# Attention steps placed relative to the next unit, and weight preparation with three raw buffers and stores issued by GpSimd

## Chip, cores and metric

One core of a Trainium2 chip runs the whole program in a single launch. The metric is the time of one execution on the device in microseconds (us). The engines are called PE (TensorE, the matrix multiplications), PEld (its weight loads), DVE (VectorE), ACT (ScalarE), POOL (GpSimd) and SP (SyncE, which issues most of the DMA transfers).

## What is computed

```python
# pooled attention: 8 batches, 8 heads, 576 positions, head size 64
k_p = k.reshape(B, H, Sp, pool, D).mean(axis=3)        # pool = 8, Sp = 72
v_p = v.reshape(B, H, Sp, pool, D).mean(axis=3)
scores = scale * np.matmul(q, k_p.transpose(0, 1, 3, 2))
scores = scores - np.max(scores, axis=-1, keepdims=True)
attn = np.exp(scores)
attn = attn / (np.sum(attn, axis=-1, keepdims=True) + 1e-09)
x = np.matmul(attn, v_p)                               # to 4608 tokens x 512
# layer 1: 512 -> 2048 -> 512
r = np.maximum(x @ w_in, 0.0)
x = (s * (r * r) + b) @ w_out
# layer 2: 512 -> 1536 -> 512
gate = 1.0 / (1.0 + np.exp(-(x @ w_gate)))
out = (gate * (x @ w_val)) @ w_out2
```

The activations are float32, the weights of the two layers float64.

## The kernel before

**Precision.** A matmul of two float32 operands is made from three: each operand is split (`split`, lines 53 to 56) into a high part, copied by ACT (line 55), and the remainder, subtracted by DVE or POOL (line 56). The float64 weights come in as pairs of 32-bit words into a tile `raw` and are turned into float32 by `convert` (lines 79 to 90): one ACT instruction (line 86) and three DVE instructions (87 to 89), into a tile `cv`.

**Tokens.** There are nine blocks of 512 tokens. Attention works in 18 units of 256 tokens, two units a block. Blocks 0, 1, 2, 4 and 6 go through layer 1 in the *plain stage*: 80 steps, 16 chunks of hidden features for each block. Blocks 3, 5, 7, 8 go through layer 1 in two *paired stages* of two blocks each, in which seven products replace eight (the scheme of Winograd, with sums of weights and of activations made beforehand). Layer 2 then has four paired stages of 1024 tokens and a last narrow one of 512 (products of 256 columns).

**The plain stage** (lines 636 to 663). Step i has two half-steps, positions 2i and 2i + 1. The first runs its events, then the 12 matmuls of `emit_h` (into PSUM tile `hps`, lines 215 to 217); the second runs its events, then the 12 matmuls of `emit_x` (into `acc`, lines 243 to 245). What the events are is written out by hand with `at(position, function, ...)` in lines 476 to 521 and kept in order of insertion. From step 16 on PE and SP execute strictly in the order of the program; before that, and on ACT, DVE and POOL throughout, a planner orders the instructions before the run by a simulation of its own, and each engine's queue is then executed in that order. Unit u begins at

```python
    def pos(u):
        return (2, 16)[u - 2] if u < 4 else 32 + 39 * (u - 4) // 5
```

so that from unit 4 on units begin 8 half-steps apart, and every fifth time 7. For a unit that begins at p, `scores` of its first 128 tokens stand at p, of the second 128 at p + 4, each as two calls with a PSUM tile `sps` each (line 379, read by DVE, lines 386 and 387). `norm` (DVE and POOL) and `left` follow. `turn` transposes the probabilities with two PSUM tiles, `tm` (line 431) and `tl` (line 437): for the first 128 tokens at p + 6, for the second at p + 9. `values` multiplies by the pooled values in two halves, PSUM tile `pv` (lines 449 to 452), at p + 11 and p + 12. A half is read by ACT and DVE, which split it in place into `xh` and `xl` (line 463) where the block stays in the plain stage, or by ACT alone, which copies it into `xo` (line 457) where the block goes to a paired stage. `sps`, `tm`, `tl` and `pv` come all from the pool `ps_c`, which has two buffers that are used in turn.

**Preparation of weights.** `prep_w1` reads a chunk of layer 1's converted weights from `w6d`, lets POOL make the four sums (lines 197 to 200) and stores them: 8 chunks, all in the plain stage, at positions 40 + 8m and 44 + 8m. `prep_w2` does a chunk of layer 2 in five parts: load gate and value weights; convert the gate weights; convert the value weights and let POOL make four sums (line 181); load the output weights; convert and split them. Each part leaves its stores in a list `later`, which `store_later` issues on SP afterwards (line 149). The raw tile of the gate weights holds the sums, that of the output weights the split ones, so they are free only when their store has landed. Four chunks (`EARLY`) are done in the plain stage with three raw tiles, at 42 + 20m and every four positions from there. The other eight are done in the paired stages of layer 1 with two raw tiles: `prep_next(1)` (lines 677 to 681) is called after each half of a group and at every fourth step of what follows, 40 times in all, one part each.

**Paired stages** (lines 818 to 865). A group has 7 products of 6 matmuls: four in `first_half` (`pb` and `pc` in PSUM, additions `add2` on DVE into `wk`, line 714), three in `second_half`, then the second layer's products into `acc` (line 804). The weights of a group, tile `w`, are fetched by SP (line 692, two buffers) from `w6d` or `w7d` when the group two before it has ended, and split by ACT and POOL (lines 55, 56). A paired stage of layer 1 has 8 groups and then 16 further steps of 12 matmuls for its second block; `gen_x` meanwhile prepares the activations of the next stage, with loads that POOL issues (line 601). In these stages PE alone is in the program's order.

## Time and profile before

| | |
|---|---|
| runs of the kernel (us) | 1794.96, 1791.48, 1795.73; median 1794.96 |
| the profiled execution's own time (us) | 1793.3 |
| its span, first to last instruction (us) | 1791.4 |
| busy (us): PE, PEld, DVE, ACT, POOL | 1726.3, 1440.6, 999.9, 874.5, 689.4 |
| mean granted clock of TensorE | 0.984 of full speed |
| first product of the first and second paired stage of layer 1, of layer 2 (us) | 635.33, 800.33, 972.74 |
| moved by DMA | 347.01 MB, 194 GB/s in the mean |

A matmul is pipelined: its busy time overlaps the next one's, so the pace is read from the starts. A wait that the profile lists is idle time of an engine, put down to the instruction whose signal came last. Idle time counts for the end only where PE, which is busy for 96% of the span, has it.

### The profile page before, as it was taken

To read this page: it belongs to the slowest core of one execution; us is meant where nothing else is said; L and a number is where in the kernel's file an instruction comes from. 1 tells how busy PE (TensorE), PEld (TensorE's weight loads), DVE (VectorE), ACT (ScalarE), POOL (GpSimd) and SP (SyncE) were. 2 spreads that over 40 slices of the span, in tenths; PEclk is the share of its full clock that TensorE was granted. 3 is DMA by queue.
4 is the path that set the end of the run, shared out by engine and by line. 5 is a ranking of instruction groups with operands and counts; after the bars stand their busy time and mean duration, and the time that the engine had idled before them with its cause. 6 is when DMAs were issued, how large, how long until landed. Compare 5 with 4: busy or idle time off the path is not lost.

```text
span 1791.4 us, 22829 instructions
## 1 busy us (share of the span) xinstructions
PE 1726.3 (96%) x8184; PEld 1440.6 (80%) x8184; DVE 999.9 (56%) x1621; ACT 874.5 (49%) x1628; POOL 689.4 (38%) x756
## 2 busy tenths in 40 slices
PE   5889999999999999999999999999999999999999
PEld 4777788787788887887788888888888888888898
DVE  7997546655533477468636545454545444554354
ACT  2667555555555676536544444344434443444244
POOL 3664335455201065425431443143314331433264
PEclk7999999999999999999999999999999999999999
DMA  6866467878334477497557333733373337333753
GB/s 237 295 231 223 170 210 276 308 258 306 125 128 129 133 267 259 169 321 259 196 194 272 108 115 139 254 112 118 137 255 114 118 135 256 115 118 130 255 183 121
DMA packets 99457, 347.01 MB, mean 194 GB/s; under 512 B 11408, under 2 KB 16528, under 8 KB 99344
## 3 DMA queue, kind: packets, MB, share of 16 engines
q1 hardware_dynamic: 95120, 331.92, 53.2%
q0 software_dynamic: 4224, 13.64, 2.4%
q8 instruction: 65, 1.06, 0.2%
q14 instruction: 48, 0.39, 0.1%
HBM read 278.40 MB, written 67.11 MB: 193 GB/s over the span
## 4 chain that ended last, share of the span: by engine, by line
PE 56%; DMA 2%; DVE 1%; POOL 1%; issue 1%; ACT 0%; SPq 0%; POOLq 0%; ACTq 0%; DVEq 0%
PE acc L804 24%; PE pc L708 6%; PE pc L709 6%; PE pc L710 6%; PE pb L710 4%; PE pb L709 4%; PE pb L708 4%; DMA raw<-in 1%; DMA w<-w7d 1%; POOL w L56 1%; DMA w<-w6d 0%; DMA w7d<-raw 0%; DVE wk L714 0%; POOL raw L181 0%; DVE cv L89 0%
## 5 line engine op out<-in xcount | busy, mean ns | idle before, releaser
L56 POOL TENSOR_TENSOR w<-w 128x256 fp32r<-128x256 f32 (+1 forms) x380 | 372.8, 1015 | 601.1 <-ACT w L55 590.1
L714 DVE TENSOR_TENSOR wk<-pc,wk 128x512 f32<-128x512 f32 (+1 forms) x304 | 196.4, 646 | 320.7 <-PE pc L710 320.0
L708 PE MATMUL pc<-xo,w 128*128 128x512 f32 (+1 forms) x608 | 227.9, 375 | 4.7 <-DVE wk L714 4.4
L709 PE MATMUL pc<-xo,w 128*128 128x512 f32 (+1 forms) x608 | 227.0, 373 | 0.0
L710 PE MATMUL pc<-xo,w 128*128 128x512 f32 (+1 forms) x608 | 226.9, 373 | 0.0
L55 ACT ACTIVATE w<-w 128x256 fp32r<-128x256 f32 (+1 forms) x380 | 157.6, 491 | 107.5 <-DMA w<-w7d 91.8
L56 DVE TENSOR_TENSOR gl<-g,gh 128x512 fp32r<-128x512 f32 (+1 forms) x172 | 132.6, 771 | 103.7 <-ACT gh L55 97.3
L708 PE MATMUL pb<-xo,w 128*128 128x512 f32 (+1 forms) x456 | 170.0, 373 | 2.2 <-ACT g L737 2.0
L710 PE MATMUL pb<-xo,w 128*128 128x512 f32 (+1 forms) x456 | 170.2, 373 | 1.4 <-POOL w L56 1.4
L709 PE MATMUL pb<-xo,w 128*128 128x512 f32 (+1 forms) x456 | 169.7, 372 | 0.0
L55 ACT ACTIVATE gh<-g 128x512 fp32r<-128x512 f32 (+1 forms) x172 | 105.7, 615 | 124.3 <-DVE g L729 121.8
L804 PE MATMUL acc<-wo,s 128*128 128x512 f32 x648 | 149.7, 389 | 0.0
L804 PEld LDWEIGHTS acc<-wo,s 128*128 128x128 f32 x648 | 121.4, 188 | 25.8 <-ACT eo L810 0.4
L708 PEld LDWEIGHTS pc<-xo,w 128*128 128x128 f32 x608 | 114.9, 189 | 27.8 <-DVE wk L714 7.7
L215 PE MATMUL hps<-xl,wi 128*128 128x512 f32 (+1 forms) x328 | 133.3, 407 | 3.5 <-ACT wi L55 2.5
L804 PE MATMUL acc<-wo,gh 128*128 128x512 f32 x432 | 133.1, 389 | 0.0
L243 PE MATMUL acc<-gl,wo 128*128 128x512 f32 x320 | 130.0, 406 | 2.0 <-DVE gl L56 1.8
L710 PEld LDWEIGHTS pc<-xo,w 128*128 128x128 f32 x608 | 114.9, 189 | 20.2
L709 PEld LDWEIGHTS pc<-xo,w 128*128 128x128 f32 x608 | 115.0, 189 | 19.6
L216 PE MATMUL hps<-xh,wi 128*128 128x512 f32 (+1 forms) x328 | 129.4, 395 | 0.0
L217 PE MATMUL hps<-xh,wi 128*128 128x512 f32 (+1 forms) x328 | 129.4, 395 | 0.0
L245 PE MATMUL acc<-gh,wo 128*128 128x512 f32 x320 | 126.5, 395 | 0.0
(123 smaller groups left out, 3410.4 us busy)
## 6 DMA issues: line engine op xcount, KB each, us to landing
wo<-wo2d SPq DMA_DIRECT2D x108, 512.0 KB, 3.5
w<-w7d SPq DMA_DIRECT2D x60, 896.0 KB, 4.4
raw<-in SPq DMA_DIRECT2D x68, 512.0 KB, 5.1
wi<-w1d SPq DMA_DIRECT2D x64, 512.0 KB, 3.9
wo<-wo1d SPq DMA_DIRECT2D x64, 512.0 KB, 4.9
w<-w6d SPq DMA_DIRECT2D x16, 896.0 KB, 5.4
kv<-in SPq DMA_DIRECT2D x24, 512.0 KB, 6.3
kv<-in SPq DMA_DIRECT2D x16, 576.0 KB, 7.3
```

The costliest lines, as they stand in the source:

```text
L55: nc.scalar.activation(out=hi, in_=src, func=ACTF.Copy)
L56: eng.tensor_tensor(out=lo, in0=src, in1=hi.bitcast(F32), op=ALU.subtract)
L215: nc.tensor.matmul(out=ps[:, f], lhsT=hi[:, kk], rhs=c[:, kk, f], start=kk == 0, stop=False)
L216: nc.tensor.matmul(out=ps[:, f], lhsT=hi[:, kk], rhs=a[:, kk, f], start=False, stop=False)
L217: nc.tensor.matmul(out=ps[:, f], lhsT=lo[:, kk], rhs=a[:, kk, f], start=False, stop=kk == KD - 1)
L243: nc.tensor.matmul(out=acc[j][d], lhsT=hi[:, f], rhs=gl, start=m == 0, stop=False)
L245: nc.tensor.matmul(out=acc[j][d], lhsT=lo[:, f], rhs=gh, start=False, stop=m == M1 - 1)
L708: nc.tensor.matmul(out=ps, lhsT=w[:, 0, x, kk], rhs=r[:, 1, kk, :n], start=first and kk == 0, stop=False, skip_group_check=True)
L709: nc.tensor.matmul(out=ps, lhsT=w[:, 0, x, kk], rhs=r[:, 0, kk, :n], start=False, stop=False, skip_group_check=True)
L710: nc.tensor.matmul(out=ps, lhsT=w[:, 1, x, kk], rhs=r[:, 0, kk, :n], start=False, stop=kk == 1, skip_group_check=True)
L714: nc.vector.tensor_tensor(out=o, in0=ps, in1=b_, op=ALU.add)
L804: nc.tensor.matmul(out=a, lhsT=l, rhs=r, start=m == 0 and first == 0, stop=m == M - 1 and first == 2)
```

## The change

The attention steps of a unit u from 4 on are placed by the beginning of unit u + 1: the second `turn` at pos(u + 1) + 1, the halves of `values` at pos(u + 1) + 3 and + 5. For units 2 and 3 the second half of `values` moves from p + 12 to p + 13. `prep_w2` is taken apart into `prep_load`, `prep_gate`, `prep_val` and `prep_out`. In the plain stage one chunk of layer 2 follows two of layer 1 in a period of 22 half-steps. In the paired stages there are three raw tiles, `wk` has nine buffers instead of ten, a chunk takes four calls (33 in all), its loads are issued two calls or more before they are converted, and POOL issues the 32 stores directly after the work that they store.

```diff
--- before.py
+++ after.py
@@ -164,41 +164,49 @@
 
     prep = {}
 
-    def prep_w2(m, part):
+    def prep_load(m, what):
+        if m < M2:
+            prep[what] = load64({"g": w_gate, "v": w_val, "o": w_out2}[what][m])
+
+    def prep_gate(m):
+        prep["gt"] = convert(prep["g"], cv_tile())
+
+    def prep_val(m):
         h0, h1 = slice(0, 256), slice(256, 512)
+        gt, vt, r = prep["gt"], convert(prep["v"], cv_tile()), prep["g"].bitcast(F32)
+        s1, s2, s3, s4 = (r[:, 256 * x:256 * x + 256] for x in range(4))
+        for o, a, b_, op in ((s1, vt[:, h0], vt[:, h1], ALU.add), (s2, s1, gt[:, h0], ALU.subtract),
+                             (s3, gt[:, h0], vt[:, h0], ALU.subtract), (s4, gt[:, h1], s2, ALU.subtract)):
+            nc.gpsimd.tensor_tensor(out=o, in0=a, in1=b_, op=op)
+        stores((w7d[m][:, 512:1024], gt), (w7d[m][:, 0:512], vt), (w7d[m][:, 1024:2048], r))
+
+    def prep_out(m):
+        t = prep["o"].rearrange("p (two f) -> p two f", two=2)
+        split(t[:, 0].bitcast(F32R), t[:, 1].bitcast(F32R), convert(prep["o"], cv_tile()), nc.gpsimd)
+        stores((wo2d[m], t))
+
+    in_pairs = []
+
+    def stores(*pairs):
+        if not in_pairs:
+            later.extend(pairs)
+            return
+        for dst, t in pairs:
+            nc.gpsimd.dma_start(out=dst, in_=t if t.dtype == F32 else t.bitcast(F32))
+
+    def prep_w1(m, part):
+
         if part == 0:
-            prep["g"] = load64(w_gate[m])
-            prep["v"] = load64(w_val[m])
-        elif part == 1:
-            prep["gt"] = convert(prep["g"], cv_tile())
-            later.append((w7d[m][:, 512:1024], prep["gt"]))
-        elif part == 2:
-            gt, vt, r = prep["gt"], convert(prep["v"], cv_tile()), prep["g"].bitcast(F32)
-            later.append((w7d[m][:, 0:512], vt))
-            s1, s2, s3, s4 = (r[:, 256 * x:256 * x + 256] for x in range(4))
-            for o, a, b_, op in ((s1, vt[:, h0], vt[:, h1], ALU.add), (s2, s1, gt[:, h0], ALU.subtract),
-                                 (s3, gt[:, h0], vt[:, h0], ALU.subtract), (s4, gt[:, h1], s2, ALU.subtract)):
-                nc.gpsimd.tensor_tensor(out=o, in0=a, in1=b_, op=op)
-            later.append((w7d[m][:, 1024:2048], r))
-        elif part == 3:
-            prep["o"] = load64(w_out2[m])
-        else:
-            t = prep["o"].rearrange("p (two f) -> p two f", two=2)
-            split(t[:, 0].bitcast(F32R), t[:, 1].bitcast(F32R), convert(prep["o"], cv_tile()), nc.gpsimd)
-            later.append((wo2d[m], t))
-
-    def prep_w1(m, part):
-
-        if part == 0:
-            prep["w"] = rawp.tile([128, 1024], I32, tag="raw", name="raw").bitcast(F32)
-            nc.sync.dma_start(out=prep["w"], in_=w6d[m][:, 0:1024])
+            prep[m] = rawp.tile([128, 1024], I32, tag="raw", name="raw").bitcast(F32)
+            nc.sync.dma_start(out=prep[m], in_=w6d[m][:, 0:1024])
             return
-        v0, v1, g0, g1 = (prep["w"][:, 256 * x:256 * x + 256] for x in range(4))
+        w = prep.pop(m)
+        v0, v1, g0, g1 = (w[:, 256 * x:256 * x + 256] for x in range(4))
         nc.gpsimd.tensor_tensor(out=v1, in0=v0, in1=v1, op=ALU.add)
         nc.gpsimd.tensor_tensor(out=v0, in0=g0, in1=v0, op=ALU.subtract)
         nc.gpsimd.tensor_tensor(out=g0, in0=v1, in1=g0, op=ALU.subtract)
         nc.gpsimd.tensor_tensor(out=g1, in0=g1, in1=g0, op=ALU.subtract)
-        later.append((w6d[m][:, 1024:2048], prep["w"]))
+        later.append((w6d[m][:, 1024:2048], w))
 
     g_t = {}
 
@@ -506,19 +514,25 @@
             if t == 0:
                 at(p + 6, turn, u, 0, 0)
                 at(p + 6, turn, u, 0, 1)
-        at(p + 9, turn, u, 1, 0)
-        at(p + 9, turn, u, 1, 1)
+        later_p = p + 8 if u < 4 else pos(u + 1)
+        at(later_p + 1, turn, u, 1, 0)
+        at(later_p + 1, turn, u, 1, 1)
         at(p + 8, load_q, u + 2)
-        at(p + 11, values, u, 0)
-        at(p + 12, values, u, 1)
-
-    for m in range(M1 // 2):
-        for x in range(2):
-            at(40 + 8 * m + 4 * x, prep_w1, m, x)
+        at(later_p + 3, values, u, 0)
+        at(later_p + 5, values, u, 1)
+
     EARLY = M2 // 3
     for m in range(EARLY):
-        for x in range(5):
-            at(42 + 20 * m + 4 * x, prep_w2, m, x)
+        p = 40 + 22 * m
+        for x in range(2):
+            at(p + 2 * x, prep_w1, 2 * m + x, 0)
+            at(p + 2 * x + 4, prep_w1, 2 * m + x, 1)
+        at(p + 8, prep_load, m, "g")
+        at(p + 8, prep_load, m, "v")
+        at(p + 12, prep_gate, m)
+        at(p + 13, prep_load, m, "o")
+        at(p + 15, prep_val, m)
+        at(p + 19, prep_out, m)
 
     def probs(u, t):
         scores(u, t, 0, True)
@@ -670,15 +684,16 @@
         w7p = ctx.enter_context(tc.tile_pool(name="w7p", bufs=2, reuse_waits="tile"))
         wo2p = ctx.enter_context(tc.tile_pool(name="wo2p", bufs=4, reuse_waits="tile"))
         g2p = ctx.enter_context(tc.tile_pool(name="g2p", bufs=1, reuse_waits="tile"))
-        wk = ctx.enter_context(tc.tile_pool(name="wk", bufs=10, reuse_waits="tile"))
-        rawp = ctx.enter_context(tc.tile_pool(name="rawp2", bufs=2, reuse_waits="tile"))
-        prepare = [(m, x) for m in range(EARLY, M2) for x in range(5)]
-
-        def prep_next(n):
-            store_later()
-            for m, x in prepare[:n]:
-                prep_w2(m, x)
-            del prepare[:n]
+        wk = ctx.enter_context(tc.tile_pool(name="wk", bufs=9, reuse_waits="tile"))
+        rawp = ctx.enter_context(tc.tile_pool(name="rawp2", bufs=3, reuse_waits="tile"))
+        in_pairs.append(1)
+        prepare = [[(prep_load, EARLY, x) for x in "gvo"]]
+        for m in range(EARLY, M2):
+            prepare += [[(prep_gate, m)], [(prep_val, m)], [(prep_load, m + 1, "g")], [(prep_out, m), (prep_load, m + 1, "v"), (prep_load, m + 1, "o")]]
+
+        def prep_next():
+            for fn, *args in prepare.pop(0) if prepare else []:
+                fn(*args)
 
         w7, wo2, g2 = {}, {}, {}
 
@@ -833,14 +848,14 @@
                 for x in new(m):
                     fetch_wo((p, 0, x))
                 half = first_half(p, m)
-                prep_next(1)
+                prep_next()
                 while len(ready) >= 2:
                     outputs(ready.pop(0))
                 if m == G - 1 and kept:
                     fetch_wo(kept.pop(0))
                     fetch_wo(kept.pop(0))
                 second_half(p, m, *half)
-                prep_next(1)
+                prep_next()
                 ready += new(m)
                 if m < G - 1:
                     fetch_w7(part + 2)
@@ -856,7 +871,7 @@
             for m in range(rest):
                 split_kept(p, m + 2)
                 if m % 4 == 0:
-                    prep_next(1)
+                    prep_next()
                 emit_o(p, m, 1)
                 wo2.pop((p, 1, m))
                 if kept:
```

## Rows read from the trace of the kernel before

**Rows 1.** The page: busy time of the engines; granted clock in 40 slices.

```profile
PE 1726.3 (96%) x8184; PEld 1440.6 (80%) x8184; DVE 999.9 (56%) x1621; ACT 874.5 (49%) x1628; POOL 689.4 (38%) x756
...
PEclk7999999999999999999999999999999999999999
```

**Rows 2.** Stages in windows: length, busy time (instructions) of each engine, clock, DMA share, GB/s.

```profile
160.00:595.00 435.00, 418.12 (x2160) 351.88 (x2159) 217.93 (x411) 239.23 (x424) 155.95 (x194) 0.99 0.59 205
635.33:800.33 165.00, 164.12 (x721) 134.90 (x720) 111.73 (x158) 94.94 (x166) 75.80 (x74) 1.00 0.74 254
800.33:972.74 172.41, 166.61 (x721) 135.73 (x720) 111.47 (x158) 94.11 (x163) 68.89 (x68) 0.99 0.68 234
972.74:1152.40 179.66, 179.66 (x794) 148.60 (x792) 89.43 (x134) 73.08 (x140) 59.82 (x68) 1.00 0.45 155
...
450.00:500.00 50.00, 45.96 (x232) 38.92 (x232) 23.91 (x48) 26.46 (x49) 9.83 (x13) 0.93 0.39 136
```

**Rows 3.** Waits of PE, 160 to 595 us: total us, times, longest us.

```profile
PE sps L379 <- DVE xl L56: 11.6, 6, 4.0
PE sps L379 <- ACT xo L457: 2.1, 6, 0.4
```

**Rows 4.** Timeline of PE: start, us, what [idle before it and releaser].

```profile
439.28 0.28 PE L452 MATMUL pv<-t,v 128*128 128x256 f32 x1
...
473.83 0.28 PE L452 MATMUL pv<-t,v 128*128 128x128 f32 x1
...
478.69 1.30 PE L379 MATMUL sps<-kbd,qT 128*128 128x144 f32 x4 [4.04 <-DVE xl L56]
479.62 0.80 PE L215 MATMUL hps<-xl,wi 128*128 128x512 f32 x1
...
484.13 0.40 PE L243 MATMUL acc<-gl,wo 128*128 128x512 f32 x1
```

**Rows 5.** Timeline of PE, 212 to 218 us.

```profile
212.63 0.50 PE L243 MATMUL acc<-gl,wo 128*128 128x512 f32 x1
...
217.08 0.22 PE L449 MATMUL pv<-t,v1h 128*128 128x128 f32 x1
```

**Rows 6.** Timeline of DVE: the writes of `xl`.

```profile
442.28 0.69 DVE L56 TENSOR_TENSOR xl<-pv,xh 128x512 fp32r<-128x512 f32 x1
...
477.86 0.69 DVE L56 TENSOR_TENSOR xl<-pv,xh 128x512 fp32r<-128x512 f32 x1
```

**Rows 7.** Waits of PE, 634 to 974 us.

```profile
PE pc L708 <- DVE wk L714: 4.4, 3, 2.8
```

**Rows 8.** The chain that ended last, 855 to 864 us: start, us, what.

```profile
856.74 4.28 DMA raw<-in
...
861.54 0.61 DVE wk L714
...
862.19 0.80 PE pc L708
```

**Rows 9.** DMA issues, 600 to 975 us: count, KB each, median us to landing.

```profile
w<-w6d SPq DMA_DIRECT2D x16, 896.0 KB, 5.4
raw<-in SPq DMA_DIRECT2D x24, 512.0 KB, 4.3
...
w7d<-raw SPq DMA_DIRECT2D x8, 512.0 KB, 4.7
```

**Rows 10.** DMA issues of POOL at line 601: ns min/median/max, first and last start.

```profile
L601 POOL DMA_DIRECT2D cv<-x2d x40: 536/536/556, 931.9 to 1673.1; - x40
```

**Rows 11.** Instruction groups of POOL and ACT, 635 to 974 us: busy us, mean ns, idle before.

```profile
L56 POOL TENSOR_TENSOR w<-w 128x512 fp32r<-128x512 f32 x34 | 46.1, 1378 | 91.9 <-ACT w L55 91.9
...
L55 ACT ACTIVATE w<-w 128x512 fp32r<-128x512 f32 x33 | 19.0, 623 | 17.7 <-DMA w<-w6d 15.7 <-DMA w<-w7d 2.0
```

**Rows 12.** Windows of the instructions on `raw` alone: DVE, ACT, POOL, clock, DMA.

```profile
635.00:710.00 75.00, 22.18 (x28) 7.94 (x12) 16.09 (x15) 1.00 0.78 266
710.00:775.00 65.00, 1.00 (x1) 0.00 (x0) 0.00 (x0) 1.00 0.62 213
```

## The prediction

> **What bounds the kernel now.** I read the page's engine line first: PE is busy 1726.3 us of the span, and the granted clock is in its top tenth in all slices but the first [rows 1]. So time can only come from the places where PE stands still or runs at half clock, and the stage table says where these are [rows 2]. Layer 2 is the yardstick: 792 matmuls of 512 columns in 179.66 us, PE busy throughout, 0.2268 us each. A paired stage of layer 1 has 8 x 42 + 2 x 16 x 12 = 720 of them, 163.3 us at that rate. The first takes 165.0 and the second 172.41: they lose 1.7 and 9.1 us, 10.8 together. The plain stage from 160 to 595 us has PE busy for 418.12 of 435 us. The first 160 us and the last narrow stage lose time too, but the change hardly touches them.
>
> The waits of PE in the plain stage have one main entry: `sps`, the scores, waits for a reader of `pv`: 11.6 us in 6 waits where the block is split in place (`xl`, line 56), 2.1 us in 6 where it is only copied (`xo`, line 457) [rows 3]. Twelve waits, about one for each unit: that is a pattern of the order, not chance. Scores and values share the two PSUM buffers of `ps_c` in turn. With `pos` 8 half-steps apart, the second values half of unit u stands at p + 12, which is the next unit's p' + 4, where its second scores stand too; values come first, so the second score tile needs the buffer that the values have just filled. With 7 apart it is the first values half that lands there. The longest case is in the timeline: last values matmul at 473.83, score tile four matmuls later, then 4.04 us of idle until `xl` has been written, 477.86 + 0.69 [rows 4, 6].
>
> Some of these waits cost twice. After the 4.04 us one, twelve matmuls take from 479.62 to 484.13, 4.51 us instead of 2.72; after a shorter one, 212.63 to 217.08, 4.45 us [rows 4, 5]. The mean granted clock from 450 to 500 us is 0.93 [rows 2], that is some 7 us at the lower of its two levels, 1.2 GHz, and PE had stood idle just before. The two cost 1.8 + 1.7 = 3.5 us.
>
> In the paired stages PE waits 4.4 us for `wk` [rows 7]. The chain shows the cause: a load of `raw` of 4.28 us, the conversion's line 87 on VectorE, behind it in the same queue the `wk` addition, then `pc` at 862.19 [rows 8]. VectorE waits in order for a raw load that could only start when a store had given the buffer free. Both stages do their sixteen half-group preparations early: `raw` is worked on for 22.18 us of VectorE in 635 to 710 us and 1.00 us in 710 to 775 [rows 12], so the static order runs them at the pace of the loads.
>
> **The change, part by part.**
>
> *Values and the last turn moved.* Values halves now stand at p' + 3 and p' + 5, the turn at p' + 1; scores have p' and p' + 4, the other turn p' + 6. No half-step has values and scores together any more. Removed: 11.6 + 2.1 = 13.7 us of waits and 3.5 us of half clock, 17.2. What is late next: the second score tile at p' + 4 now needs the first values half of p' + 3, and the small transpose at p' + 6 needs the second half of p' + 5. Each has one half-step of twelve matmuls (2.72 us) and about 0.5 us of its neighbours before it, 3.2 us. How long an eviction takes, from the end of the last values matmul to the end of `xl`: 474.11 to 478.55 is 4.4 us, 439.56 to 442.97 is 3.4 [rows 4, 6]; a copied block never waits over 0.4 us [rows 3], so its evictions are shorter. So 1.2 + 0.2 us stay, and for six split units meeting a conversion's VectorE work I add 1 us: 2.5 back. Bounds: nothing gained if every wait only changes its place, 17.2 if none stays. I take -14.7, near the upper end, since only two of the evictions read exceed 3.2 us. For units 2 and 3 only the second values half moves, by one half-step, in a stretch where PE's order is not written by hand: between -2.7 and +2.7 us, taken as 0.
>
> *Early preparation laid out anew.* The same 8 `w6d` loads, 12 weight loads, 24 stores and conversions, now one after the other instead of two interleaved series, each read four half-steps or more after its load (4 x 2.72 = 10.9 us, against the 4.3 us that a raw load takes to land in the paired stages [rows 9]). All still goes through SP. None of its work ended a wait of PE in the list of the plain stage [rows 3], except through VectorE's queue, counted above. 0, with a half-step, 2.7 us, to either side.
>
> *Three raw buffers and the new steps.* Each load now stands two calls or more ahead of its conversion, with a buffer of its own. Program order has 7.5 us between calls, so two calls are 15 us. The tightest is the gate: the store of the sums must land (4.7 us) and then the load (4.3 us): 9.0 us [rows 9]. At the program's pace that fits and the 10.8 us go. But the present order runs these calls in 75 us instead of 120 [rows 12], that is 4.7 us each, and two of those are 9.4: hardly any margin. The bounds are 0 and -10.8 (a loss is a rival below). I take -6, just over half: of three loads per chunk two have ample lead and one hasn't.
>
> *Stores from GpSimd.* 8 chunks x 4 = 32 stores leave SP's queue, where they stood ahead of the raw loads. GpSimd issues its own loads in 536 ns, without spread [rows 10]: 32 x 0.54 = 17 us of an engine that is busy 75.80 + 68.89 of 337 us [rows 2]. No cost, as long as GpSimd's weight splits stay in time. Their slack: `w` lands 5.4 us after its fetch [rows 9], ScalarE's 0.62 and GpSimd's 1.38 us follow [rows 11], 7.4 us before the first product, out of a group of 66 x 0.2268 = 15.0 us. So GpSimd may be held for 7.6 us.
>
> The Trainium skill, "SBUF — State Buffer", in "SBUF: two separate sides" and the section on the wrong bandwidth intuition behind it, says that a DMA issued by GpSimd can't have its descriptors written while VectorE runs an operation that takes both ports, and gives 620 ns alone against about 3100 ns beside one. By that, 32 stores would hold GpSimd for 99 us, an estimate from the page. No run here shows it: the 40 issues of that row end at 556 ns, and few lie beside a conversion.
>
> *`wk` with nine buffers.* A group uses six, so a buffer comes round after one and a half groups, 22 us; the readers are done within one. 0. The third raw buffer takes its space.
>
> *Sum.* -14.7 - 6 = -20.7 us. The profiled execution took 1793.3 us (span 1791.4 and 1.9 around it), which gives 1772.6. The median of the runs is 1.7 us above that execution, so I forecast **1774 us**.
>
> **The rivals.**
>
> *Only the half-steps help.* The static order again follows the loads as closely as it can, and VectorE's queue meets unfinished loads as before. For: preparation packed into 75 us. Against: a third buffer and no store in the loads' queue. 1795 - 14.7 = 1780 us.
>
> *Only the preparation helps.* The waits for `pv` pass to the transposes and to the second scores, which also share `ps_c`. For: the two evictions over 3.2 us. Against: all others are shorter. 1795 - 6 to - 11 = 1784 to 1789 us.
>
> *Nothing to measure.* Both of these fail, or the gain is given back in the reordered first 160 us: 1790 to 1800 us.
>
> *Slower: GpSimd becomes late.* The place is the weight split of line 56 in layer 1, behind stores and their data in GpSimd's queue. It decides when GpSimd is held for more than 7.6 us after a group's fetch. A sum that waits for VectorE's conversion, three more sums behind it and the stores of their result, held until VectorE leaves the ports free, could do that. If half of the 16 groups come 4 us late, PE loses 32 us, and 1774 + 32 + the 6 us not gained is 1812 us. For: GpSimd's queue is in order, and it already waits for ScalarE. Against: it is idle for over half of these stages. A smaller excess gives 1801 or so.
>
> **How the numbers follow.** About 0.3%, 5.4 us, is what a measurement of this kernel can tell from no change. Chances: the forecast, with its own range of 1763 to 1780 us, 0.47; half-steps alone 0.20; preparation alone 0.12; nothing 0.12; slower 0.09. The first three lie under 1789.6: faster 0.79, same 0.12, slower 0.09. The range reaches from 1763, by 1795 - 17.2 - 10.8 - 3 = 1764, where every wait goes and the early stretch gives 3 us more, to 1788, leaving out the last two cases.
>
> **What would show it.** Right: in the list of PE's waits the entries `sps` on `xl` and `xo` are gone or under 3 us; the half-clock stretches near 213 and 480 us are missing; the first pair stage begins about 15 us earlier; the second takes nearer to 166 than 172 us; GpSimd's stores stay near 0.54 us. Wrong: `tl` or `sps` waiting for `pv` readers with 10 us or more, `pc` waiting for `wk` behind line 87 as before, or `pb` waiting for GpSimd's line 56 in layer 1.

## The result, and the profile after

The changed kernel takes 1777.85 us in the median of four runs (1777.2 to 1779.04), the kernel before 1795.35 (1791.48 to 1798.54): a ratio of 0.9904, 95% interval 0.9884 to 0.9925. The forecast was 1774 us, within 1763 to 1788, faster. The profiled execution took 1777.24 us (span 1775.4, mean clock 0.988), 16.1 us less than that of before.

The stages in windows, kernel after; the columns are those of [rows 2], and the windows of the paired stages again run from first product to first product:

```profile
160.00:595.00 435.00, 429.70 (x2236) 363.20 (x2235) 230.15 (x433) 253.87 (x452) 156.22 (x197) 1.00 0.63 215
613.51:783.12 169.61, 165.79 (x722) 134.44 (x721) 121.50 (x166) 96.25 (x168) 88.84 (x97) 1.00 0.73 254
783.12:955.10 171.98, 165.63 (x722) 136.04 (x721) 104.20 (x150) 92.66 (x161) 70.92 (x77) 0.99 0.67 226
955.10:1135.02 179.92, 179.83 (x793) 148.61 (x792) 88.94 (x134) 73.13 (x140) 60.34 (x68) 1.00 0.45 155
```

The same 435 us of the plain stage now hold 429.70 us of busy PE instead of 418.12, and the granted clock is 1.00 instead of 0.99. The first product of the paired stages comes at 613.51 us, 21.8 us earlier than the 635.33 of before. That is the whole gain and more. The two paired stages of layer 1 take 169.61 + 171.98 = 341.6 us instead of 337.4, so 4.2 us are lost where the forecast had a gain of 6. The rest is small: 1.8 us more in the four stages of layer 2, 0.2 us less after them. -21.8 + 4.2 + 1.8 - 0.2 = -16.0, the difference of the two spans.

The 21.8 us have two parts. The first scores of unit 4 begin at 168.05 us instead of 171.74, 3.7 us that the start of the program has given. In the experiments below that moment lies between 168.1 and 171.0 us wherever the half-steps are changed, and at 172.0 us in the one kernel where they are not: some 1.7 us of it go with the half-steps (the second values half of units 2 and 3 has moved too), the rest is scatter. From there to the first paired product it is 445.5 us instead of 463.6, 18.1 us less. This stretch in windows (columns of [rows 2]), first of the kernel before, then of the kernel after:

```profile
171.74:635.33 463.59, 446.71 (x2281) 375.44 (x2280) 231.06 (x432) 258.69 (x459) 159.21 (x200) 0.99 0.58 203
```

```profile
168.05:613.51 445.46, 440.16 (x2281) 371.89 (x2280) 228.68 (x432) 257.75 (x459) 157.88 (x200) 1.00 0.62 212
```

For the same 2281 matmuls PE stands idle for 5.3 us instead of 16.9, and its busy time is 6.5 us shorter. The waits of PE, 160 to 595 us, kernel after (as in [rows 3]: total, times, longest):

```profile
PE tm L439 <- DVE e L395: 2.3, 2, 1.3
PE sps L387 <- ACT t L446: 1.8, 1, 1.8
PE sps L387 <- DVE t L56: 1.1, 1, 1.1
```

Both entries of [rows 3] are gone, all twelve waits, and nothing in the list waits for a reader of `pv`. These three entries come to 5.2 us; beside the two of [rows 3] the list of before has two others, 3.0 us together:

```profile
PE tm L431 <- DVE e L387: 1.6, 2, 0.8
PE sps L379 <- DVE t L56: 1.4, 2, 1.1
```

In the paired stages, 613 to 974 us, the wait of [rows 7] has grown:

```profile
PE pc L723 <- DVE wk L729: 8.9, 7, 3.0
PE pb L723 <- ACT g L752: 1.1, 1, 1.1
```

PE waits twice as long for VectorE's additions as before (for ScalarE's `g` it waited 2.0 us before, 634 to 974 us). Yet what the change aimed at happened. The waits of VectorE for raw loads, 605 to 975 us, first of the kernel before, then of the kernel after:

```profile
DVE raw L87 <- DMA raw<-in: 27.1, 12, 5.6
```

```profile
DVE raw L87 <- DMA raw<-in: 17.9, 8, 4.9
```

VectorE waits 9 us less for loads, and PE 4.5 us more for VectorE. So the raw load wasn't what the time hung on, or something else has taken its place; it turns out to be some of both.

### The profile page after: what moved, and what is told of

The parts are those of the page before. It is cut to its first block, busy times and chain, and to the rows that moved or that the text cites. A ratio compares the mean times of both kernels' runs of the same rounds, so it can differ in the third digit from the quotient of the medians.

```text
span 1775.4 us, 22857 instructions
## 1 busy us (share of the span) xinstructions
PE 1718.1 (97%) x8184; PEld 1435.0 (81%) x8184; DVE 996.1 (56%) x1621; ACT 873.2 (49%) x1628; POOL 702.8 (40%) x788
## 4 chain that ended last, share of the span: by engine, by line
PE 53%; DMA 4%; DVE 2%; issue 2%; POOL 2%; ACT 0%; DVEq 0%; POOLq 0%; SPq 0%; ACTq 0%
PE acc L819 20%; PE pc L723 6%; PE pc L724 6%; PE pc L725 6%; PE pb L725 5%; PE pb L724 5%; PE pb L723 5%; DMA wo<-wo2d 1%; DMA raw<-in 1%; POOL w L56 1%; DMA cv<-x1d 1%; POOL raw L180 1%; DVE raw L87 0%; DMA wo2d<-raw 0%; DVE cv L88 0%
## 5 line engine op out<-in xcount | busy, mean ns | idle before, releaser
L723 PE MATMUL pb<-xo,w 128*128 128x512 f32 (+1 forms) x456 | 169.9, 373 | 1.4 <-ACT g L752 1.1
```

The lines of the kernel that those rows point to most:

```text
L723: nc.tensor.matmul(out=ps, lhsT=w[:, 0, x, kk], rhs=r[:, 1, kk, :n], start=first and kk == 0, stop=False, skip_group_check=True)
```

## The experiments

My theory after this result: the half-steps give all of the gain, the preparation in the paired stages costs some 4 us, and the question is which of its parts. The rivals were the new layout in the plain stage, VectorE's planned order, the number of conversions, the loads' order and GpSimd's stores. In all of the kernels PE's order in the paired stages is the same, so the time of 8 groups less 8 x 66 x 0.2268 = 119.8 us is what PE loses in them. The table has the results: the length of the two stages, what PE loses in the groups of each, the number of VectorE instructions over 1.9 us in both (with their sum in us), and the ratio of the times.

| kernel | stages, us | groups lose, us | over 1.9 us | ratio (95% interval) |
|---|---|---|---|---|
| before | 165.0 + 172.4 | 1.7 + 9.1 | 0 | 1 |
| changed | 169.6 + 172.0 | 6.3 + 8.7 | 3 (9.7) | 0.9904 (0.9884 to 0.9925) |
| changed_again | 171.9 + 169.9 | 7.1 + 6.6 | 3 (9.6) | 0.9896 (0.9877 to 0.9915) |
| halfsteps | 165.3 + 173.1 | 1.3 + 8.4 | 0 | 0.9865 (0.9838 to 0.9892) |
| prep_only | 177.9 + 167.7 | 7.0 + 4.4 | 4 (11.8) | 1.0011 (0.9996 to 1.0026) |
| old_pairs | 166.2 + 170.5 | 1.6 + 6.6 | 0 | 0.9858 (0.9840 to 0.9876) |
| sp_stores | 176.4 + 171.5 | 12.6 + 7.1 | 0 | 0.9899 (0.9878 to 0.9919) |
| dve_order | 218.1 + 202.5 | 34.6 + 26.6 | 0 | 1.0297 (1.0274 to 1.0320) |
| five_calls | 169.9 + 170.3 | 5.2 + 7.0 | 4 (10.7) | 0.9883 (0.9867 to 0.9900) |
| three_raw | 167.0 + 168.6 | 3.4 + 5.2 | 0 | 0.9855 (0.9837 to 0.9873) |
| gp_stores | 173.7 + 177.9 | 8.9 + 14.0 | 10 (31.2) | 0.9957 (0.9940 to 0.9974) |
| five_sp | 167.7 + 170.0 | 3.6 + 6.7 | 0 | 0.9868 (0.9850 to 0.9886) |
| early6 | 169.7 + 171.2 | 3.1 + 7.9 | 0 | 0.9891 (0.9874 to 0.9908) |
| five_act | 168.8 + 171.3 | 4.5 + 8.0 | 0 | 0.9861 (0.9833 to 0.9889) |

Four blocks (halfsteps, prep_only, old_pairs and sp_stores; changed_again, dve_order, five_calls and three_raw; gp_stores, five_sp and early6; five_act) ran on one chip each, beside the kernel before, whose medians there were 1799.99, 1798.80, 1797.59 and 1799.21 us. The stages and the losses are read from one profile of each kernel. The two profiles of the changed kernel differ by 1.3 us in the losses, so differences of 1 or 2 us between kernels tell nothing.

**halfsteps: the kernel before with the attention part alone.**

```diff
-        at(p + 9, turn, u, 1, 0)
-        at(p + 9, turn, u, 1, 1)
+        later_p = p + 8 if u < 4 else pos(u + 1)
+        at(later_p + 1, turn, u, 1, 0)
+        at(later_p + 1, turn, u, 1, 1)
...
-        at(p + 11, values, u, 0)
-        at(p + 12, values, u, 1)
+        at(later_p + 3, values, u, 0)
+        at(later_p + 5, values, u, 1)
```

> Only the attention half-steps of the change. Theory (the whole gain of the plain stage comes from them): the first product of the paired stages comes at about 614 us as in the changed kernel, the two paired stages of layer 1 take 165 and 172 us as before, and the time is about 1774 us. Rival (the new layout of the early preparation gave part of the plain stage's 21.8 us): the first product comes at 618 to 628 us, the time is 1778 to 1788 us.

1774.86 us. The first product comes at 616.24 us, and the paired stages are as long as before. These few lines are worth 1.35%, at least as much as the whole change (0.96%; the two intervals overlap).

**prep_only: the changed kernel with these lines taken back.**

> Only the preparation (its new layout in the plain stage, three raw buffers, new steps and GpSimd's stores in the paired stages); attention as before. Theory (the preparation gives nothing in the plain stage and loses 4 us in the paired ones): first product at 633 to 638 us, paired stages of layer 1 at 340 to 343 us together, time 1797 to 1801 us. Rival (it shares in the plain stage's gain): first product at 622 to 630 us, time 1786 to 1794 us.

1800.93 us beside 1799.99. First product at 638.04 us, no gain in the plain stage. Its waits there, 160 to 595 us, are the old ones:

```profile
PE sps L387 <- DVE xl L56: 11.3, 6, 4.7
PE sps L387 <- ACT xo L465: 2.5, 7, 0.4
```

The paired stages take 345.6 us, longer than expected, 7.7 us of it lost after the groups of the first stage, where PE waits 3.4 us for a load of `wo` and runs at half clock for some 7 us around it. The time agrees with the theory; the length of the stages overshoots it.

**old_pairs: the changed kernel with the paired stages' preparation of before.**

```diff
-        wk = ctx.enter_context(tc.tile_pool(name="wk", bufs=9, reuse_waits="tile"))
-        rawp = ctx.enter_context(tc.tile_pool(name="rawp2", bufs=3, reuse_waits="tile"))
-        in_pairs.append(1)
+        wk = ctx.enter_context(tc.tile_pool(name="wk", bufs=10, reuse_waits="tile"))
+        rawp = ctx.enter_context(tc.tile_pool(name="rawp2", bufs=2, reuse_waits="tile"))
+        prepare = [(m, x) for m in range(EARLY, M2) for x in range(5)]
...
```

> The changed kernel with the paired stages' preparation of before (two raw buffers, ten wk buffers, forty calls, stores by SP). Theory (what the change does in the paired stages is a loss of about 4 us): first product at 613 to 615 us, the two paired stages of layer 1 together 337 us instead of 341.6, time 1773 to 1775 us. Rival (their length follows from how they are entered, not from this part): together 340 to 344 us, time 1777 to 1780 us.

1774.41 us, 336.7 us for the stages, as the theory has it. The first product comes at 615.23 us: against 616.24 of the half-steps alone, the new layout in the plain stage is worth 1 us at most, which is within the scatter of that moment (611.4 to 615.7 in the kernels with the half-steps and a new layout).

**sp_stores: the changed kernel with its stores issued by SP, at the same places.**

```diff
-            nc.gpsimd.dma_start(out=dst, in_=t if t.dtype == F32 else t.bitcast(F32))
+            nc.sync.dma_start(out=dst, in_=t if t.dtype == F32 else t.bitcast(F32))
```

> The changed kernel with the 32 stores of the paired stages issued by SP at the same places. Theory A (GpSimd's stores hold GpSimd and VectorE, and cause the loss): the two paired stages of layer 1 together 330 to 337 us, time 1768 to 1774 us. Theory B (the loss comes from VectorE's order, conversions queued ahead of the additions that PE waits for, whoever stores): 339 to 345 us together, time 1776 to 1782 us. Theory C (stores that wait for their data hold SP's fetches): over 345 us, time over 1782 us.

347.8 us: over the bound of theory C, though the time, 1781.72 us, still lies in B's. SP's queue, 605 to 975 us, kernel sp_stores:

```profile
SPq L195 <- DVE cv L89: 46.1, 13, 7.9
...
SPq L195 <- POOL raw L180: 17.2, 6, 3.6
...
SPq L195 <- POOL raw L56: 13.1, 6, 7.2
```

Line 195 is the store, line 73 the raw load. SP's stores wait for VectorE and GpSimd, 76 us in all, with the raw loads behind them. The sum doesn't set this kernel apart: stores that are left to the next call, as in the kernel before, wait as long there (line 149, 78 us). But theory C's mechanism can be seen at PE's longest wait. SP, VectorE and PE:

```profile
688.51 0.33 SPq L195 DMA_DIRECT2D w7d<-cv  x1
688.94 0.37 SPq L73 DMA_DIRECT2D raw<-in  x1
```

```profile
693.84 0.43 DVE L87 TENSOR_SCALAR raw<-raw 128x512 int32<-128x512 int32 x1 [4.75 <-DMA raw<-in]
```

```profile
695.52 0.79 PE L723 MATMUL pc<-xo,w 128*128 128x512 f32 x1 [4.45 <-DVE wk L729]
```

The store has waited 7.9 us for VectorE's conversion, the raw load follows it in the queue and lands at 693.74 us, VectorE stands idle until then, and PE until the addition behind it. So this kernel has a cost of its own, and it leaves open what GpSimd's stores cost by themselves.

**changed_again: the changed kernel once more, beside the next three.**

> The changed kernel, unaltered, beside the next three on one chip. All theories: a ratio to the kernel before near 0.990, the two paired stages of layer 1 at 339 to 344 us together (341.6 in its first profile), first product near 614 us.

1780.03 us, 341.8 us in the stages: the loss of 4 us is no accident of one profile.

**dve_order: VectorE in the order of the program in the two stages.**

```diff
+        dve_order = ExitStack()
+        dve_order.enter_context(tc.manual_schedule(engines={mybir.EngineType.DVE}))
         fetch_w7(0)
         fetch_w7(1)
...
+            if p == 2:
+                dve_order.close()
```

> The changed kernel with VectorE in the order of the program in the paired stages of layer 1, so that a conversion stands where its call stands, between the additions of two half-groups. Theory A (the loss comes from the planned order, which bunches conversions ahead of additions that PE waits for): the two stages fall to 327 to 333 us together, the ratio to 0.982 to 0.985. Theory B (VectorE has too much work for these groups in any order): 338 us or more, ratio 0.988 or more. Theory C (waits for ScalarE in a fixed order cost more than they save): over 345 us.

1851.71 us. Theory A's forecast fails, and C holds: VectorE waits 91.5 us for ScalarE's `gh` (613 to 1040 us) where the changed kernel has 8.8 (613 to 974 us). The program's order is far worse than the planner's. That the planner's order costs nothing doesn't follow, since this one brings waits of its own. Waits of PE, 613 to 1040 us, kernel dve_order:

```profile
PE pc L723 <- DVE wk L729: 42.0, 17, 6.1
PE acc L819 <- DVE gl L56: 23.6, 2, 13.8
```

**five_calls: five calls for a chunk instead of four.**

```diff
-            prepare += [[(prep_gate, m)], [(prep_val, m)], [(prep_load, m + 1, "g")], [(prep_out, m), (prep_load, m + 1, "v"), (prep_load, m + 1, "o")]]
+            prepare += [[(prep_gate, m)], [(prep_val, m)], [(prep_load, m + 1, "g")], [(prep_out, m)], [(prep_load, m + 1, "v"), (prep_load, m + 1, "o")]]
```

> The changed kernel with five calls for a chunk instead of four (the loads of value and output weights get a call of their own), so that conversions are spread over all forty calls as before. Theory A (the chunks come too densely: five chunks' conversions meet the first stage's groups instead of four): the two stages at 333 to 338 us together, nearer to the 338.4 of the half-steps alone or below, ratio 0.986 to 0.988. Theory B (the planner bunches them whatever the calls): 340 to 344 us, ratio 0.990.

340.1 us, which is theory B's, and a ratio of 0.9883, which lies between the two: 1.7 us less in the stages than with four calls, too little to tell.

**three_raw: old_pairs with three raw buffers and nine of wk.**

```diff
-        wk = ctx.enter_context(tc.tile_pool(name="wk", bufs=10, reuse_waits="tile"))
-        rawp = ctx.enter_context(tc.tile_pool(name="rawp2", bufs=2, reuse_waits="tile"))
+        wk = ctx.enter_context(tc.tile_pool(name="wk", bufs=9, reuse_waits="tile"))
+        rawp = ctx.enter_context(tc.tile_pool(name="rawp2", bufs=3, reuse_waits="tile"))
```

> Half-steps and the plain stage's layout as changed, the paired stages' steps and SP stores of before, but with three raw buffers and nine of wk. Theory A (a third buffer frees the loads, the new steps and stores are what costs): the two stages at 328 to 334 us together against 336.7 with two buffers, ratio 0.982 to 0.985. Theory B (the third buffer is worth nothing, since the loads still stand behind stores in SP's queue): 335 to 339 us, ratio 0.986.

1771.9 us, 0.9855 where the changed kernel has 0.9896 on the same chip, and the two intervals don't meet. It is the shortest time, though old_pairs, five_act, halfsteps and five_sp can't be told from it. But against two buffers (0.9858) the stages gain 1 us, theory B. VectorE's waits for raw loads, 605 to 975 us, first old_pairs, then three_raw:

```profile
DVE raw L87 <- DMA raw<-in: 26.0, 11, 6.4
```

```profile
DVE raw L87 <- DMA raw<-in: 13.7, 7, 4.4
```

They are halved by the third buffer, and the groups lose 8.6 us instead of 8.2. This is the plainest answer to the forecast's -6: the raw waits can be had away without PE gaining by it. What PE waits for instead shows in its five waits for `wk` (4.6 us). None stands directly behind an idle wait of VectorE for a load; ahead of each addition VectorE runs the instructions of a conversion (lines 87 to 89), in one case after waiting 1.1 us for its step on ScalarE. The longest, VectorE and then PE, kernel three_raw:

```profile
822.07 1.04 DVE L88 SCALAR_TENSOR_TENSOR cv<-cv,raw 128x512 int32<-128x512 int32 x1
823.14 1.10 DVE L89 SCALAR_TENSOR_TENSOR cv<-raw,cv 128x512 int32<-128x512 int32 x1
824.16 0.68 DVE L751 TENSOR_TENSOR wk<-pc,wk 128x512 f32<-128x512 f32 x1
```

```profile
824.89 0.50 PE L745 MATMUL pc<-xo,w 128*128 128x512 f32 x1 [1.64 <-DVE wk L751]
```

**gp_stores: three_raw with its stores issued by GpSimd right behind the work.**

```diff
-            later.append((wo2d[m], t))
+            stores((wo2d[m], t))
...
+        in_pairs.append(1)
```

(so for all four stores of a chunk)

> The kernel with three raw buffers and the paired stages' five steps of before (1771.9 us, losses of 3.4 and 5.2 us in the groups of the two stages), with one part of the change put back: the stores issued by GpSimd right behind the work. Theory A (GpSimd's stores cost nothing and free the loads): losses of 3 to 9 us in both stages together, ratio 0.984 to 0.986. Theory B (stores on GpSimd hold its splits and VectorE's conversions): 11 to 16 us together, ratio 0.988 to 0.991.

1789.98 us. The groups lose 22.9 us instead of 8.6: over theory B's bound. GpSimd's issue of a store itself is short (0.55 us here). VectorE, and then GpSimd, of kernel gp_stores at one of these stores:

```profile
637.20 0.69 DVE L752 TENSOR_TENSOR wk<-pc,wk 128x512 f32<-128x512 f32 x1 [0.42 <-PE pc L748]
637.92 4.90 DVE L778 SCALAR_TENSOR_TENSOR g<-wk 128x512 f32<-128x512 f32 x1
642.75 0.68 DVE L752 TENSOR_TENSOR wk<-pc,wk 128x512 f32<-128x512 f32 x1
```

```profile
637.08 0.55 POOL L218 DMA_DIRECT2D w7d<-cv  x1 [5.13 <-DVE cv L89]
637.64 4.63 POOL L56 TENSOR_TENSOR w<-w 128x512 fp32r<-128x512 f32 x5
```

A VectorE instruction that takes 0.69 us elsewhere takes 4.90, and it ends 0.55 us after GpSimd's five splits behind the store (637.64 + 4.63 = 642.27, the instruction at 642.82). The kernel before has the same run of five splits, without a store ahead of it. VectorE, and then GpSimd:

```profile
662.86 3.33 DVE L740 SCALAR_TENSOR_TENSOR g<-wk 128x512 f32<-128x512 f32 x2
666.11 0.68 DVE L714 TENSOR_TENSOR wk<-pc,wk 128x512 f32<-128x512 f32 x1
```

```profile
662.63 5.55 POOL L56 TENSOR_TENSOR w<-w 128x512 fp32r<-128x512 f32 x5 [1.45 <-ACT w L55]
```

There two such instructions take 3.33 us together and GpSimd's run 5.55: each engine is slowed some. Behind a store GpSimd's run is the faster (4.63) and VectorE stands still for all of it. Each of the ten long instructions of this kernel begins within the issue of a store by GpSimd or up to 0.6 us behind its end. No kernel whose stores SP or ScalarE issues has one over 1.9 us, and each with GpSimd's has 3 to 10, but for dve_order, where VectorE mostly waits. The changed kernel and sp_stores differ in the issuer alone: 3 and 0. And PE pays for it here: of the 15.3 us that it waits in these stages, 12.7 stand directly behind a run of VectorE with one of the long instructions in it (in one wait, 3.7 us, a late conversion has its part too). No wait of PE is for GpSimd.

**five_sp: five_calls with the stores issued by SP one call later.**

```diff
-        in_pairs.append(1)
...
         def prep_next():
+            store_later()
```

> The changed kernel's early loads in five calls (losses of 5.2 and 7.0 us with GpSimd's stores), with the stores issued by SP one call later, as before the change. Theory A (the stores make the difference to the steps of before): losses of 6 to 9 us together, ratio 0.985 to 0.986. Theory B (the early loads themselves let the planner pack conversions into the first stage's groups): 11 to 16 us together with 12 or more conversions there, ratio 0.988 to 0.990.

0.9868, and 10.3 us lost, between the two theories' bounds; 12 conversions fall to the first stage, as many as in three_raw (11 in the kernel before). So with these steps GpSimd's stores cost 1.9 us (12.2 against 10.3), which can't be told from nothing, and with the old ones 14.3 (22.9 against 8.6). That it hangs on what the planner puts behind the stores is likely, but not shown. In both pairs GpSimd also stores one call earlier than SP.

**early6: three_raw with six chunks prepared in the plain stage, and three calls for two groups.**

```diff
-    EARLY = M2 // 3
+    EARLY = M2 // 2
     for m in range(EARLY):
-        p = 40 + 22 * m
-        for x in range(2):
+        p = 36 + 22 * m if m < 4 else 116 + 12 * (m - 4)
+        for x in range(2 if m < 4 else 0):
...
-                prep_next(1)
+                if m % 2:
+                    prep_next(1)
```

> Three raw buffers and the steps of before with SP's stores, but six chunks of layer 2 prepared in the plain stage instead of four (the last two at half-steps 116 to 147), so that 18 conversions instead of 24 are left for the paired stages, and three calls for two groups instead of four. Theory A (PE's loss in the groups goes with the number of conversions that VectorE has there): losses of 8.6 us in the groups fall to 2 to 5, the plain stage gets up to 2 us longer, ratio 0.981 to 0.984. Theory B (the loss is set by waits for raw loads, whatever the number): 7 to 10 us stay, ratio 0.985 to 0.987. Theory C (the plain stage loses what the paired ones gain): first product at 617 us or later, ratio 0.985 or more.

1776.97 us. The plain stage gets no longer (first product at 611.95 us), so theory C falls; but with 16 conversions in the groups instead of 22 these still lose 11.0 us, above even B's bound. The loss doesn't go with the number of conversions alone. The wait for a raw load isn't gone here either: PE's longest wait for `wk`, 3.4 us of 6.0, comes after 3.7 us in which VectorE waits for one.

**five_act: five_sp with ScalarE as the issuer.**

```diff
         def prep_next():
-            store_later()
+            while later:
+                dst, t = later.pop(0)
+                nc.scalar.dma_start(out=dst, in_=t if t.dtype == F32 else t.bitcast(F32))
```

> The changed kernel's early loads in five calls, the paired stages' stores issued by ScalarE one call later (with SP: losses of 3.6 and 6.7 us in the groups of the two stages, ratio 0.9868; with GpSimd: 5.2 and 7.0 us, 0.9883). Theory A (what GpSimd's stores cost is that VectorE is held for several of GpSimd's instructions behind each of its DMA issues): as with SP no VectorE instruction of these stages over 1.9 us, against 3 to 10 with GpSimd, and losses of 4 to 10 us together, ratio 0.984 to 0.987. Theory B (any stores off SP's queue bring such instructions): some over 1.9 us. Theory C (ScalarE, waiting for the data of a store, holds its own work for PE): none over 1.9 us, yet losses over 11 us, ratio 0.988 or more.

No VectorE instruction over 1.9 us and a ratio of 0.9861, as theory A has it, so it isn't leaving SP's queue that makes them long, it is GpSimd. The groups lose 12.5 us, though, which is C's side; but PE's waits for ScalarE (3.2 us) are hardly longer than with SP (3.0), so what C names isn't shown. Nothing is won over SP.

## Why the prediction was right, and where it was wrong

**The values and the last turn: right, the term too small.** -14.7 was forecast, -18.1 measured between unit 4's first scores and the paired stages. The removed 13.7 + 3.5 us went as worked out: no wait for `pv` readers, a clock of 1.00. The 2.5 us I gave back didn't come where I put them. The two evictions I had read as 3.4 and 4.4 us (unit 12's first half, unit 13's second) take 1.6 and 2.7 in the new place, timelines of PE and of VectorE, kernel after:

```profile
427.57 0.28 PE L460 MATMUL pv<-t,v 128*128 128x256 f32 x1
...
463.84 0.28 PE L460 MATMUL pv<-t,v 128*128 128x128 f32 x1
```

```profile
428.72 0.69 DVE L56 TENSOR_TENSOR xl<-pv,xh 128x512 fp32r<-128x512 f32 x1 [3.39 <-ACT xh L55]
...
466.08 0.69 DVE L56 TENSOR_TENSOR xl<-pv,xh 128x512 fp32r<-128x512 f32 x1
```

From 427.85 to 429.41 us, with VectorE idle for 3.39 us before the split, and from 464.12 to 466.77, with other work ahead of it. All twelve split evictions from unit 4 on take 1.4 to 2.7 us, under the 3.2 that the new places leave, so none holds PE. The half-steps alone (halfsteps) have two of 3.6 and 3.8 us, and 1.1 us of waits for them at `tl` and `sps`, the places and nearly the 1.4 us that I had worked out. What did come back is 2.2 us of other waits (5.2 against 3.0). That PE's busy time fell by 6.5 us, where I had counted 3.5 for the half clock, more than makes up for it; where the other 3 us lie isn't shown.

**The early stretch and the plain preparation: nearly as forecast.** The start gave 3.7 us in this profile, 1 us beyond the 2.7 to either side that I had allowed units 2 and 3, and some 1.7 us in the median of the kernels with these half-steps. prep_only and old_pairs show the new layout to be worth nothing that can be told.

**Three raw buffers, -6: wrong.** -6 was forecast, +4.2 measured. The step that failed is "VectorE waits in order for a raw load", taken as the cause of all of PE's 10.8 us. The chain of [rows 8] was true of that one wait, 2.8 us, and old_pairs has it again (2.8 us). But the load didn't wait for a free buffer, as I had it. The two links ahead of [rows 8] in the chain of the kernel before:

```profile
855.13 1.16 DVE cv L89
...
856.31 0.32 SPq L149
```

Line 149 is a store: it waited in SP's queue for VectorE's own conversion, and the load at 856.74 us went out right behind it, as in sp_stores. In three_raw that wait is gone and the groups lose as much, 8.6 us against 8.2, because other additions then stand behind conversions that run. Neither the program's order (dve_order) nor fewer conversions (early6) made it less. Whether another order could is open.

A third raw buffer also meets a limit that I had left out. `eo`, the output of a stage, takes its tiles from the same six `cv` buffers as the conversions. At the start of the second stage, ScalarE, VectorE and PE, kernel after:

```profile
791.03 0.66 ACT L86 ACTIVATE cv<-raw 128x512 f32<-128x512 f32 x1 [5.76 <-DMA x2d<-eo]
```

```profile
791.72 0.69 DVE L88 SCALAR_TENSOR_TENSOR cv<-cv,raw 128x512 int32<-128x512 int32 x1 [1.83 <-ACT cv L86]
```

```profile
793.07 0.79 PE L723 MATMUL pc<-xo,w 128*128 128x512 f32 x1 [2.99 <-DVE wk L729]
```

A conversion waits for the store of `eo` to land, VectorE for the conversion's step on ScalarE, and PE for the addition behind it: 2.99 us, its longest wait, and some 3 us at half clock after it. Every kernel with three raw buffers but prep_only has such a wait of ScalarE for `eo` (1.0 to 5.8 us), none with two has one.

**GpSimd's stores, 0: wrong in the sum, and the rival named another place.** I looked for the cost in GpSimd's queue, at its splits. The issue is as short as [rows 10] promised; the kernel after at line 195 (ns min/median/max):

```profile
L195 POOL DMA_DIRECT2D w7d<-cv x16: 547/570/761, 619.9 to 844.9; - x16
...
L195 POOL DMA_DIRECT2D wo2d<-raw x8: 539/557/573, 627.5 to 848.6; - x8
L195 POOL DMA_DIRECT2D w7d<-raw x8: 533/557/714, 628.1 to 849.2; - x8
```

No wait of PE in the two stages is for a split of GpSimd. What became late is VectorE. In the case that costs PE most in the changed kernel, VectorE and then GpSimd, the addition ends PE's wait of 2.83 us for `wk` at 811.34 us:

```profile
806.86 3.83 DVE L87 TENSOR_SCALAR raw<-raw 128x512 int32<-128x512 int32 x1 [0.90 <-DMA raw<-in]
810.61 0.68 DVE L729 TENSOR_TENSOR wk<-pc,wk 128x512 f32<-128x512 f32 x1
```

```profile
806.46 0.57 POOL L195 DMA_DIRECT2D wo2d<-raw  x1
807.05 3.34 POOL L56 TENSOR_TENSOR w<-w 128x512 fp32r<-128x512 f32 x4
```

This is also the sign that I had named as wrong, `pc` waiting for `wk` behind line 87, though for another reason. Of PE's 8.9 us for `wk`, 4.3 stand directly behind two such long instructions (2.83 us here, 1.48 at 659.48 us), 2.99 behind the `cv` tile, and the other 1.6 in four short waits. In the second profile (changed_again) 2.7 of 8.5 us, `pb` included, stand behind long instructions.

The rule of the Trainium skill that I had weighed ("SBUF — State Buffer", "SBUF: two separate sides" and the section on the wrong bandwidth intuition) has GpSimd's DMA held by VectorE: about 3100 ns instead of 620. The longest of the 32 issues here took 761 ns, so that half of it is not seen. The same section of the Trainium skill has a pair of ports that goes to one of the two engines for a whole instruction and blocks the other. A VectorE instruction that stands still agrees with that, but it stands through two to five of GpSimd's, not one: there the measurement decides.

**The sum.** -16.1 measured in the profiled executions against -20.7: the plain stage gave 7.1 us more than forecast, the start included, the paired stages 10.2 less, layer 2 1.8 less. That the time came within 4 us of the forecast is in part luck: two errors of opposite sign. The likeliest case wasn't what happened; by its result it was the rival "only the half-steps help", forecast at 1780 us with a chance of 0.20. That rival's reason, VectorE meeting unfinished loads as before, holds in part only: these waits fell from 27.1 to 17.9 us.

## What to carry to other kernels

Where two users of one ring of PSUM buffers fall into the same half-step, look whether the second waits for the first one's eviction. Here it did twelve times, and moving them apart was worth 18 us where the waits came to 13.7, in part because PE ran at half clock after two of them. A wait in an engine's list is worth removing only if the wait of the bound engine goes with it: halving VectorE's waits for loads gave PE nothing. Follow a late load one step further back, to what stands ahead of it in its queue: here it was a store, not a missing buffer. Stores moved to GpSimd left SP's queue, but held VectorE where the two engines worked side by side, so compare the longest VectorE instructions of both traces, not the issue's own time.

## What was not expected of the hardware

A VectorE instruction that starts during GpSimd's issue of a DMA, or within 0.6 us of its end (in one place 1.3), can be held until the run of GpSimd instructions behind that issue is nearly or quite over: 2.0 to 4.9 us for instructions that otherwise take 0.43 to 1.8, in ten places of gp_stores and three of the changed kernel, which each have 32 such issues. The 16 loads that GpSimd issues in these stages of every kernel bring none. In the two places shown, GpSimd's run of five splits takes 4.63 us behind a store, against 5.55 beside VectorE without one. Why an issue gives GpSimd the way for several instructions no run here shows. The stores themselves land no later for it: 4.5 us in the median for the sums, against 4.7 us when SP issued them [rows 9].
